# Two DFT steps along S, from 128x128 weights with masks to 32x32 tiles, in a forward and backward pass of a spectral mixer and a token MLP

## The chip, the cores and the metric

The kernel runs on one core of a Trainium2 chip (trn2), in one launch. The metric is the device time in microseconds (us), the median over several executions. TensorE is PE (its weight loads are listed as PEld), VectorE DVE, ScalarE ACT, GpSimd POOL, SyncE SP. SP issues nearly all DMAs.

## The reference

Inputs are bf16: `x` and `grad_out` of 2048 x 448 (S x D), the filter `w_r`, `w_i` of 2048 x 225, `w1` of 2048 x 1792, `w2` of 1792 x 2048, and the biases. With LN the layer norm over D:

```python
def _A_ref(x, w_r, w_i):                       # spectral filter
    X = jnp.fft.rfft2(x.astype(jnp.float32), axes=(-2, -1))
    X = X * (w_r + 1j * w_i)
    return jnp.fft.irfft2(X, s=(S, D), axes=(-2, -1)).astype(jnp.bfloat16)

def _B_ref(x, w1, b1, w2, b2):                 # MLP over the tokens
    h = LN(x)
    u = gelu(einsum("bsd,sf->bdf", h, w1) + b1)
    return (einsum("bdf,fs->bds", u, w2) + b2).transpose(0, 2, 1)

h  = x + _A_ref(LN(x), w_r, w_i)
h2 = h + _B_ref(LN(h), w1, b1, w2, b2)
# outputs: h2 and the gradients of x, w_r, w_i, w1, b1, w2, b2 for grad_out
```

## The kernel before

**Stages.** In the order of PE's work: (1) warm-up; (2) the forward DFT of LN(x) along D and the first step along S, a loop `for t in range(NT)` over 16 tiles with `row_a(t+1)` (4 matmuls of 128 columns) and `row_b(t-3)` (4 of 226); (3) `s2_stage`, the second step along S, the product with the filter and the first inverse step; (4) `inv_rows`, the rest of the inverse, and the layer norm of `h`; (5) the MLP forward and the gradients up to `dh` (the loop with `mm(pdh...)`), in which the first step of the backward DFT starts (`rows(t)`); (6) `s2_stage` again, for the gradient, with `bwd_mult`; (7) `inv_rows` again with `gx_consumer`, which makes the gradient of `x`; (8) what is left of the weight gradients.

**Fill.** Two long products have no place of their own: `dg_gen` (`w2` times `grad_out`, 224 matmuls of 448 columns) is fed into stages 2 and 3, and `gw_gen` (the gradients of `w1` and `w2`) into stages 5 to 8. Each is a Python generator; `fill(n)` emits its next n steps. A step of `dg_gen` is one matmul. Fourteen steps of `gw_gen` are twelve matmuls of 512 columns (in the last quarter of out_4, 256) and one group of four matmuls on 64 rows each (`parts`). What is left of `dg_gen` at the end of stage 3, and of `gw_gen` at the end of stage 7, is emitted there by `drain()`.

**Second step along S.** S = 16 x 128 frequencies lie in 16 groups of 128 rows. In each group the step is a 128x128 complex matrix which by the arrangement of the rows is nonzero only where a mask (`masks`, four comparisons per row) leaves it: the tables `Ut`, `Vt` are made as compact columns by ACT's Sin (`comp`), then spread over 128 columns by 16 multiplications with the mask columns (`gen_UV`). `UTt`, `VTt` are their permuted transposes, made on PE (`gen_inv_s`, 8 calls of four 128-column matmuls). In `s2_stage` a group takes three full matmuls forward and three back (`s2_inv`):

```python
mm(pv, lhsT=Vt[:, g, :], rhs=D2[:, g, :, :], start=True, stop=False)              # 452 columns
mm(pv[:, 0, :], lhsT=Ut[:, g, :], rhs=D2[:, g, 1, :], start=False, stop=False)    # 226
mm(pv[:, 1, :], lhsT=Un[g], rhs=D2[:, g, 0, :], start=False, stop=True)           # 226
evac(out=xs[c2][:, i, :, :], in_=pv, scale=scale)
```

The stage runs over pairs of groups `c2`. After each group comes `fill(n_fill)`: 3 in stage 3, 8 in stage 6. After each pair the filter product `w_mult` (4 DVE products) follows, in stage 6 also the filter's gradient (4 more). `D2` (the input of the stage) is written by 8 DMAs (L693), `D3` (its output) by one DMA per group (L756), each issued some PE time after the evacuation it stores (`defer`, `RESH_LAG`).

**Filter.** `w_load` (L583) reads `w_r`, `w_i` by eight DMAs in rows of up to 7200 bytes into `W_rows` (four in the loop of stage 2, four at the start of stage 3); `w_place` (32 copies) puts them in the order of the groups into `rG` during stage 3; a DMA stores them to DRAM (`w_d`, L963), and four DMAs (L1216) fetch them back into `rC` in stage 5. The gradient is stored from there by `w_io` (L572), eight DMAs.

**Who evacuates.** `evac` gives each PSUM tile to ACT or DVE by a planner's two loads (`Meter`, L62 to L81): each instruction adds its estimated cost, and neither load may fall behind the other by more than `Meter.slack` (2.0, in stage 6 4.0). PSUM has four buffers of the kind `ps_ff` (used by the DFTs) and four of `ps_mm` (used by the fill). PE, DVE, ACT and SP run in the order written down; POOL's order is the scheduler's.

Of the kernel before, what the change touches and what calls it, by code (L numbers as in the profile page):

```python
# [17 lines left out]
P = 128  # L18
# [104 lines left out]
def kernel(  # L123
# [98 lines left out]
    def v4(ap):  # L222
        return ap.rearrange("p (b c) -> p b c", b=4)
# [8 lines left out]
    r2 = region("r2", NG * 3 * KW)  # L232
# [3 lines left out]
    rX = region("rX", NG * 2 * KW)  # L236
    r452 = region("r452", 8 * 452)
# [4 lines left out]
    Ut = mem.tile([P, NG, P], BF16, name="Ut")  # L242
    Vt = mem.tile([P, NG, P], BF16, name="Vt")
    UTt = mem.tile([P, NG, P], BF16, name="UTt")
    VTt = mem.tile([P, NG, P], BF16, name="VTt")
# [3 lines left out]
    permI = mem.tile([P, P], BF16, name="permI")  # L249
# [35 lines left out]
    w_d = dram.tile([P, NG * 2 * KW], BF16, name="w_d")  # L285
# [70 lines left out]
    fr = ftmp(448, 64)  # L356
    gp_.iota(fr.rearrange("p (c q i g) -> p c q i g", c=2, q=2, i=4), pattern=[[1, 2], [8, 2], [16, 4], [2, 4]], base=0,
# [73 lines left out]
    def gen_R(ve, sc):  # L431
        t = ftmp(2688, P).bitcast(I32)
        tv = t.rearrange("p (c h x) -> p c h x", c=4, h=2)
        f2 = fr.rearrange("p (c x) -> p c x", c=4)
        for h in range(2):
            ve.tensor_scalar(out=tv[:, :, h, :], in0=f2, scalar1=pcol, scalar2=96.0 + 32.0 * h, op0=ALU.mult, op1=ALU.add)
        ve.tensor_scalar(out=tv[:, 0, 1, 0:1], in0=pcol, scalar1=64.0, scalar2=96.0, op0=ALU.mult, op1=ALU.add)
        ve.tensor_scalar(out=t, in0=t, scalar1=127, scalar2=None, op0=ALU.bitwise_and)
        sc.activation(out=Rm[:], in_=t, func=ACT.Sin, scale=s128, bias=half_r)


    def decode(eng):
        a4, fc, s_, c_, f_ = col(), col(), col(), col(), col()
        floor_div(eng, a4, pcolb, 32)
        gp_madd(s_, a4, -32.0, pcolb)
        floor_div(eng, fc, s_, 4)
        gp_madd(s_, fc, -4.0, s_)
        gp_madd(s_, s_, 4.0, a4)
        floor_div(eng, c_, fc, 4)
        gp_madd(f_, c_, -4.0, fc)  # L450
        return fc, s_, c_, f_

    def masks(eng, c_, f_):
        msk, mk, k0, k1 = col(4), col(), col(), col()
        for j in range(4):
            eng.tensor_scalar(out=msk[:, j:j + 1], in0=f_, scalar1=float(j), scalar2=None, op0=ALU.is_equal)
        eng.tensor_tensor(out=mk, in0=msk[:, 0:1], in1=c_, op=ALU.mult)
        eng.tensor_scalar(out=k1, in0=mk, scalar1=-1.0, scalar2=1.0, op0=ALU.mult, op1=ALU.add)
        eng.tensor_tensor(out=k0, in0=mk, in1=msk[:, 0:1], op=ALU.subtract)
        eng.tensor_scalar(out=k0, in0=k0, scalar1=1.0, scalar2=None, op0=ALU.add)  # L460
        return msk, mk, k0, k1

    comp_ring = ring(rO, 0, 2, 512)

    def gen_UV():
        _, s_, c_, f_ = rows = decode(gp_)
        nrow = col()
        gp_madd(nrow, rows[0], 16.0, s_)
        msk, mk, k0, k1 = masks(gp_, c_, f_)
        slf = col()  # L470
        gp_.tensor_tensor(out=slf, in0=s_, in1=f_, op=ALU.mult)
        gp_.tensor_scalar(out=slf, in0=slf, scalar1=16.0, scalar2=1536.0, op0=ALU.mult, op1=ALU.add)
        ou, ov0, ov1, pu, pv = col(), col(), col(), col(), col()
        gp_madd(ou, c_, 1536.0, slf)
        gp_madd(ov0, c_, -512.0, slf)
        gp_.tensor_scalar(out=ov0, in0=ov0, scalar1=512.0, scalar2=None, op0=ALU.add)
# [5 lines left out]
        ve.tensor_scalar(out=permI[:], in0=krow[:, 0:P], scalar1=nrow, scalar2=None, op0=ALU.is_equal)  # L482
        ve.scalar_tensor_tensor(out=base[:, 0, :, 1], in0=fix, scalar=mk, in1=base[:, 0, :, 1], op0=ALU.mult, op1=ALU.add)
        for dst, o0, o1, pt in ((Ut, ou, ou, pu), (Vt, ov0, ov1, pv)):
            t = ftmp(1024 if dst is Ut else 2048, 16, 16, 2).bitcast(I32)
            for k, o in ((0, o0), (1, o1)):
                ve.tensor_scalar(out=t[:, :, :, k], in0=base[:, :, :, k], scalar1=s_, scalar2=o,
                                 op0=ALU.mult, op1=ALU.add)
                yield
            ve.tensor_scalar(out=t[:, 0, :, 1], in0=base[:, 0, :, 1], scalar1=s_, scalar2=pt, op0=ALU.mult, op1=ALU.add)  # L490
# [3 lines left out]
            comp = comp_ring.next()  # L494
            sc.activation(out=comp, in_=t.rearrange("p g l c -> p (g l c)"), func=ACT.Sin, scale=s2048, bias=half_uv)
            yield True
            cv = comp.rearrange("p (g l c) -> p g l c", g=16, l=16)
            for c, k in ((1, k0), (0, k1)):
                ve.tensor_scalar(out=cv[:, 0, :, c], in0=cv[:, 0, :, c], scalar1=k, scalar2=None, op0=ALU.mult)
            yield  # L500
            d0 = dst[:, :, 0:64].rearrange("p g (l f) -> p g l f", f=4)
            d1 = dst[:, :, 64:112].rearrange("p g (l f) -> p g l f", f=3)
            for j in range(4):
                m = msk[:, j:j + 1]
                dj = d1[:, :, :, j - 1] if j else dst[:, :, 112:128]
                for o, c in ((d0[:, :, :, j], 0), (dj, 1)):
                    if load[1] + 0.24 < load[0] + 0.38:
                        ve.tensor_scalar(out=o, in0=cv[:, :, :, c], scalar1=m, scalar2=None, op0=ALU.mult)
                    else:
                        sc.activation(out=o, in_=cv[:, :, :, c], func=ACT.Copy, scale=m)  # L510
                    yield
# [7 lines left out]
    def gen_inv_s(h):  # L519
        src, dst = ((Ut, UTt), (Vt, VTt))[h // 4]  # L520
        g0 = 4 * (h % 4)
        pt = ps_ff()
        for i in range(4):
            mm(pt[:, i * P:(i + 1) * P], lhsT=src[:, g0 + i, :], rhs=permI[:], start=True, stop=True)
        evac(out=dst[:, g0:g0 + 4, :].rearrange("p g c -> p (g c)"), in_=pt[:])
# [34 lines left out]
    W_view_F = cut(rG, 0, NG, 2, KW)  # L560
    W_view_B = cut(rC, 0, NG, 2, KW)

    def w_io(Wv, dr, di, store):
        for c_, d in ((0, dr), (1, di)):
            for p0, p1, g0, g1, row, dims in ((0, 64, 0, 16, 0, [[16 * DF, 4], [1, 16 * DF]]),
                                              (64, 112, 0, 16, 112, [[-DF, 48], [1, DF]]),
                                              (112, 128, 1, 16, 127, [[-DF, 15], [1, DF]]),
                                              (112, 128, 0, 1, 64, [[1, DF]])):
                sb = Wv[p0:p1, g0:g1, c_, 0:DF]
                d_ap = bass.AP(d.tensor, d.offset + row * DF, [[P * DF, 16]] + dims)  # L570
                if store:
                    nc.sync.dma_start(out=d_ap, in_=sb)  # L572
                else:
                    nc.sync.dma_start(out=sb, in_=d_ap)
                yield

    W_rows = cut(rB, 0, 2, NG, DF)

    def w_load():
# [869 lines left out]
```

## Time and profile before

| | us |
|---|---|
| median of 3 runs | 356.51 |
| lowest, highest | 356.15, 356.75 |
| span of the profiled execution | 355.2 |
| PE busy in it | 340.1 (96%) |
| DVE busy | 253.9 (71%) |
| ACT busy | 214.9 (61%) |
| POOL busy | 69.7 (20%) |

For the profiled execution the page gives the span, from the first to the last instruction; its own time with what lies around the span is not listed apart. The three timed executions lie 1.0 to 1.6 us above it, the median 1.3 us, and that is taken as what lies around the span.

The page shows the busy time of each engine, then the span in 40 slices, then the chain of work that ended last, then the costliest groups of instructions. A matmul's own duration covers the way through the array, so matmuls overlap: what a matmul costs PE is the distance from its start to the next start, which the timeline gives. The granted clock is 1.00 in all stages.

### The profile page before, as it was taken

What the parts mean: (1) busy time and instruction counts of PE and PEld (TensorE: products, weight loads), DVE (VectorE), ACT (ScalarE), POOL (GpSimd) and SP (SyncE); (2) the same over time, 40 slices, a digit from 0 to 9 for tenths busy, and PEclk for the clock granted to TensorE, in tenths of its full rate; (3) what the DMA queues carried; (4) which work ended last, traced back from release to release, by engine and by line L of the source; (5) the groups of instructions that cost most, each with busy time, mean ns of one, the idle gap of its engine ahead of it and who ended that gap; (6) DMA issues with size and microseconds to landing.
All of it is one profiled execution on the core that took longest, in us unless ns stands there. A gap on an engine that the chain in (4) does not pass through costs nothing.

```text
span 355.2 us, 6479 instructions
## 1 busy us (share of the span) xinstructions
PE 340.1 (96%) x2147; PEld 184.2 (52%) x2147; DVE 253.9 (71%) x679; ACT 214.9 (61%) x458; POOL 69.7 (20%) x227
## 2 busy tenths in 40 slices
PE   7588999999999999999999999999999999999995
PEld 3355766555645555555555555544454544555642
DVE  8895638981884888776236988786595965499993
ACT  5469848964986545504322346666387766579872
POOL 6876000000220000001001111110000000067880
PEclk9999999999999999999999999999999999999999
DMA  8999979768999999997876999969966898799995
GB/s 196 284 190 244 212 186 184 139 170 279 285 288 352 297 350 230 246 235 213 209 171 149 184 219 190 206 158 304 295 177 193 231 233 248 230 198 284 209 303 221
DMA packets 147673, 81.64 MB, mean 230 GB/s; under 512 B 95480, under 2 KB 139768, under 8 KB 147384
## 3 DMA queue, kind: packets, MB, share of 16 engines
q1 hardware_dynamic: 147352, 80.83, 91.9%
q8 instruction: 17, 0.28, 0.3%
q10 hardware_dynamic: 288, 0.39, 0.3%
q14 instruction: 16, 0.13, 0.1%
HBM read 27.56 MB, written 23.89 MB: 145 GB/s over the span
## 4 chain that ended last, share of the span: by engine, by line
PE 82%; ACT 6%; POOL 5%; DVE 4%; issue 2%; DVEq 0%; ACTq 0%; POOLq 0%
PE ps_mm L218 68%; PE ps_ff L218 14%; ACT rO L82 2%; DVE r L82 1%; ACT rG L82 1%; ACT Ut L82 1%; DVE rA L82 1%; POOL cols L406 1%; POOL cols L407 0%; DVE rG L82 0%; ACT rX L82 0%; ACT rD L82 0%; ACT rAT L82 0%; ACT csI L82 0%; POOL nt_f L385 0%
## 5 line engine op out<-in xcount | busy, mean ns | idle before, releaser
L218 PEld LDWEIGHTS <-r 128*128 128x128 bf16 (+1 forms) x660 | 61.8, 104 | 50.0 <-issue 3.0
L218 PEld LDWEIGHTS <-rS 128*128 128x128 bf16 (+2 forms) x496 | 40.1, 97 | 37.8 <-issue 4.9
L218 PE MATMUL ps_mm<-rD,r 128*128 128x448 bf16 x224 | 44.5, 352 | 0.0
L82 ACT CAST rO<-ps_mm 128x512 bf16<-128x512 f32 (+1 forms) x66 | 35.2, 579 | 11.3 <-PE ps_mm L218 10.8
L218 PEld LDWEIGHTS <-rst 128*128 128x128 bf16 (+1 forms) x320 | 23.8, 97 | 29.0 <-issue 13.7
L218 PE MATMUL ps_mm<-rC,rE 128*128 128x448 bf16 x144 | 33.4, 352 | 3.2 <-DMA rC<-in_grad_out_dram 3.2
L218 PE MATMUL ps_mm<-r,rst 128*128 128x512 bf16 (+3 forms) x192 | 36.5, 353 | 0.0
L82 ACT CAST r<-ps_ff 128x452 bf16<-128x452 f32 x55 | 31.3, 577 | 7.3 <-PE ps_ff L218 6.2
L218 PE MATMUL ps_mm<-rB,r 128*128 128x448 bf16 x160 | 31.2, 352 | 0.1
L218 PE MATMUL ps_mm<-rG,rst 128*128 128x512 bf16 (+1 forms) x128 | 28.4, 380 | 0.0
L82 ACT ACTIVATE r<-ps_mm,rstd_h 128x448 bf16<-128x448 f32 x16 | 10.1, 634 | 26.8 <-PE ps_mm L218 26.8
L82 ACT ACTIVATE r<-rC 128x448 bf16<-128x448 bf16 x16 | 9.1, 570 | 26.7 <-DMA out_dram<-r 21.8
L82 DVE SCALAR_TENSOR_TENSOR r<-ps_mm,b2col,r 128x448 bf16<-128x448 f32 x16 | 10.9, 682 | 19.9 <-PE ps_mm L218 18.3
L82 ACT ACTIVATE rG<-rG 128x896 bf16<-128x896 bf16 x14 | 13.3, 950 | 14.9 <-DVE rG L82 14.7
L218 PE MATMUL ps_mm<-rE,rS 128*128 128x448 bf16 x112 | 21.5, 352 | 0.0
L218 PEld LDWEIGHTS <-rO 128*128 128x128 bf16 (+1 forms) x165 | 15.7, 98 | 10.9 <-ACT rO L82 0.2
L1179 POOL TENSOR_SCALAR lcol<-lcol 128x1 f32<-128x1 f32 x16 | 8.5, 532 | 64.7 <-ACT r L82 64.7
L82 ACT CAST rS<-ps_ff 128x512 bf16<-128x512 f32 x30 | 17.7, 592 | 4.3 <-PE ps_ff L218 4.3
L1370 POOL TENSOR_SCALAR lcol<-lcol 128x1 f32<-128x1 f32 x16 | 4.6, 287 | 76.5 <-ACT r L82 76.4
L218 PEld LDWEIGHTS <-rE 128*128 128x128 bf16 x148 | 14.0, 98 | 10.6 <-issue 3.7
L218 PE MATMUL ps_ff<-csI,rAT 113*128 113x224 bf16 (+1 forms) x108 | 19.0, 297 | 0.4 <-ACT rAT L82 0.2
L82 ACT CAST rG<-ps_mm 128x512 bf16<-128x512 f32 (+1 forms) x28 | 14.4, 550 | 8.1 <-PE ps_mm L218 8.0
(196 smaller groups left out, 667.0 us busy)
## 6 DMA issues: line engine op xcount, KB each, us to landing
out_dram<-rO SPq DMA_DIRECT2D x34, 256.0 KB
r<-in_B_w_dram SPq DMA_DIRECT2D x5, 1024.0 KB
r<-r SPq DMA_DIRECT2D x16, 226.0 KB
r<-r SPq DMA_DIRECT2D x32, 113.0 KB
rS<-in_B_w_dram SPq DMA_DIRECT2D x4, 896.0 KB
out_dram<-rG SPq DMA_DIRECT2D x10, 256.0 KB
rO<-in_B_w_dram SPq DMA_DIRECT2D x2, 1024.0 KB
w_d<-rG SPq DMA_DIRECT2D x1, 1808.0 KB
```

The source lines that it names most:

```text
L82: fn(**kw)
L218: nc.tensor.matmul(out, lhsT=lhsT, rhs=rhs, start=start, stop=stop)
L406: gp_.tensor_scalar(out=gtmp, in0=in0, scalar1=scalar, scalar2=None, op0=ALU.mult)
L1179: gp_.tensor_scalar(out=m1, in0=ms, scalar1=-1.0 / D, scalar2=None, op0=ALU.mult)
L1370: gp_.tensor_scalar(out=m1, in0=ms, scalar1=-2.0 / D, scalar2=None, op0=ALU.mult)
```

## The change

The rows are arranged in such a way that the second step's matrix is block diagonal in blocks of 32 within each group. The tables are 32 columns wide and need no masks (`masks` and its 16 multiplications are gone; the angles get two more DVE operations, `bi`). `s2_stage` takes the groups in four sets of four. For each of the three tables a set issues 16 matmuls with 32x32 weights, one for each block row r and each group a; group a's block r lands in rows r + a (modulo 4), so that the 16 use all 16 places of the array. Forward, `fill(n1)`, back for the set before, product, `fill(n2)` follow for each set. The filter is loaded in place into a tile of its own, `rW`, by `w_io` (18 DMAs with rows of 450 bytes, all in the loop of stage 2) and stays there, so that `w_place`, `w_d` and the four loads are gone; its gradient is stored by the same 18 patterns. `gen_inv_s` is 4 calls of 32 small matmuls. The fill is dealt out anew. The diff, cut to its core:

```diff
+    def small(out, lhsT, rhs, start, stop):
+        nc.tensor.matmul(out, lhsT=lhsT, rhs=rhs, start=start, stop=stop)
+        clock[0] += int(np.prod(rhs.shape[1:])) / 38400.0
+    def blk(i):
+        return slice(32 * i, 32 * i + 32)
+    def set_groups(s):
+        return [8 * (s // 2) + s % 2 + 2 * a for a in range(4)]
...
+    Ut, Vt, Un, UTn = (mem.tile([P, NG, 32], BF16, name=n) for n in ("Ut", "Vt", "Un", "UTn"))
+    UVT = mem.tile([P, 2, NG, 32], BF16, name="UVT")
...
     def gen_UV():
...
+        ve.tensor_scalar(out=bi, in0=base, scalar1=i16, scalar2=None, op0=ALU.add)
+        ve.tensor_scalar(out=bi, in0=bi, scalar1=2047 - 64, scalar2=None, op0=ALU.bitwise_and)
+        yield
...
-            for j in range(4):
-                m = msk[:, j:j + 1]
-                dj = d1[:, :, :, j - 1] if j else dst[:, :, 112:128]
-                for o, c in ((d0[:, :, :, j], 0), (dj, 1)):
-                    if load[1] + 0.24 < load[0] + 0.38:
-                        ve.tensor_scalar(out=o, in0=cv[:, :, :, c], scalar1=m, scalar2=None, op0=ALU.mult)
-                    else:
-                        sc.activation(out=o, in_=cv[:, :, :, c], func=ACT.Copy, scale=m)
-                    yield
...
-        for i in range(4):
-            mm(pt[:, i * P:(i + 1) * P], lhsT=src[:, g0 + i, :], rhs=permI[:], start=True, stop=True)
+        for w, src in enumerate((Ut, Vt)):
+            for x in range(4):
+                o = 32 * (4 * w + x)
+                for r in range(4):
+                    small(pt[blk(r + a & 3), o:o + 32], lhsT=src[blk(r), 8 * (x // 2) + 2 * a + x % 2, :], rhs=permI[blk(r), :],
+                          start=True, stop=True)
...
+    def w_io(dr, di, store):
         for c_, d in ((0, dr), (1, di)):
+            for i in range(4):
+                for p0, g0, g1, row, dims in ((0, 0, 16, 16 * i, [[DF, 16], [1, DF]]),
+                                              (16, 0 if i else 1, 16, 128 - 16 * i - (not i), [[-DF, 16 if i else 15], [1, DF]]),
+                                              (16, 0, 1, 64, [[1, DF]])):
+                    if i and row == 64 and g1 == 1:
+                        continue
+                    p0 += 32 * i
+                    sb = W[p0:p0 + 16, g0:g1, c_, 0:DF]
+                    d_ap = bass.AP(d.tensor, d.offset + row * DF, [[P * DF, 16]] + dims)
+                    nc.sync.dma_start(out=d_ap if store else sb, in_=sb if store else d_ap)
                     yield
...
+    def s2_stage(get_x, on_mult, n1, n2, gap, after=None, scale=None):
         flush()
+        def four(tables, s, turn, rhs):
+            gs = set_groups(s)
+            ps = [ps_ff()[:, 0:452].rearrange("p (c k) -> p c k", c=2) for _ in gs]
+            for t, c, start, stop in ((tables[0], None, True, False), (tables[1], 0, False, False), (tables[2], 1, False, True)):
+                for a, g in enumerate(gs):
+                    for r in range(4):
+                        x, o = rhs(a, g, r), ps[a][blk(r + turn * a & 3)]
+                        small(o if c is None else o[:, c, :], lhsT=t[blk(r), g, :], rhs=x if c is None else x[:, 1 - c, :],
+                              start=start, stop=stop)
+            run_due()
+            return ps
+        y = None
+        for s in range(5):
+            if s < 4:
+                x = get_x(s)
+                for a, pv in enumerate(four((Vt, Ut, Un), s, 1, lambda a, g, r: D2[blk(r), g])):
+                    evac(out=x[:, a], in_=pv, scale=scale)
+            fill(n1)
+            if s:
+                for g, pv in zip(set_groups(s - 1), four((VTt, UTt, UTn), s - 1, -1, lambda a, g, r: y[blk(r), a])):
+                    ab = r452_ring.next()
+                    evac(out=ab, in_=pv)
+                    defer(RESH_LAG, lambda g=g, ab=ab: nc.sync.dma_start(out=D3[rowbase(g):rowbase(g) + 29:4, :, :, :], in_=ab), ab)
+            if s < 4:
+                y = Y_ring.next()
+                for j in range(2):
+                    on_mult(s, j, x[:, 2 * j:2 * j + 2], y[:, 2 * j:2 * j + 2])
+            if after is not None and s in after:
+                after[s]()
+            fill(n2)
         fill(gap)
...
-    FILL_A = (4, 4, 4, 3, 3, 4, 4, 4, 4, 4, 4, 3, 3, 3, 3, 3)
-    FILL_B = (0, 0, 0, 3, 3, 3, 3, 3, 3, 3, 3, 3, 3, 3, 3, 3)
+    W_AT = {4: 1, 5: 1, 6: 1, 7: 1, 8: 2, 9: 2, 10: 2, 11: 2, 12: 2, 13: 2, 14: 2}
+    FILL_A = (4, 4, 4, 3, 3, 3, 3, 3, 3, 3, 3, 3, 3, 3, 3, 3)
+    FILL_B = (0, 0, 0, 2, 2, 2, 2, 2, 2, 2, 2, 2, 2, 2, 2, 2)
...
-    wp = w_place()
-    fill(14)
+    gen_inv_d(0)
+    fill(6)
+    gen_inv_d(1)
...
-    s2_stage(fwd_x, fwd_mult, ML_F, 3, 24, True)
+    s2_stage(lambda s: set_of(Xs, s), fwd_mult, 10, 14, 0)
+    sc.activation(out=warm, in_=eps_h, func=ACT.Sqrt)
+    fill(24)
     drain()
-    nc.sync.dma_start(out=w_d[:], in_=rG[:, 0:NG * 2 * KW])
...
-    s2_stage(bwd_x, bwd_mult, 0, N_FILL_B[3], N_FILL_B[4], False, {5: lambda: load_du(0), 9: lambda: load_du(1), 13: lambda: load_du(2)}, 2.0 * INV_SD)
+    s2_stage(lambda s: X_ring.next(), bwd_mult, 14, 22, N_FILL_B[4], {1: lambda: load_du(0), 3: lambda: (load_du(1), load_du(2))},
+             2.0 * INV_SD)
...
-    GW_AT = (1, 3, 5, 6, 7, 9, 11, 12)
+    GW_AT = tuple(range(1, 13)) + tuple(range(6, 12))
```

In the changed program the planner deals the evacuations of stage 6 as follows: in DVE's queue, between the products of one set and those of the next, stand one or two evacuations of the set's forward step, two of the fill, and one or two of the back step of the set before; before the first set's products stand three forward ones and two of the fill. In stage 3 two of the four back evacuations of each set stand on DVE between the products of two sets; the forward ones are on ACT but for two of the first set.

## The prediction

> **What bounds the kernel now.** I read, in this order: the page's shares, the slices, the chain, then PE's timeline at the step that changes, and the queues around it.
>
> ```profile
> PE 340.1 (96%) x2147; PEld 184.2 (52%) x2147; DVE 253.9 (71%) x679; ACT 214.9 (61%) x458; POOL 69.7 (20%) x227
> PE   7588999999999999999999999999999999999995
> PE 82%; ACT 6%; POOL 5%; DVE 4%; issue 2%; DVEq 0%; ACTq 0%; POOLq 0%
> ```
>
> PE is busy 96% of the span, its slices are full from the fifth on, and 82% of the chain is PE. So what is taken from PE's own time shortens the run, unless a queue that PE's time used to cover comes out. PE's timeline shows one group of the second step, then the fill:
>
> ```profile
> 49.74 0.35 PE L218 MATMUL ps_ff<-r,Vt 128*128 128x452 bf16 x1
> 49.93 0.26 PE L218 MATMUL ps_ff<-r,Ut 128*128 128x226 bf16 x1
> 50.02 0.26 PE L218 MATMUL ps_ff<-r,r 128*128 128x226 bf16 x1
> 50.12 0.35 PE L218 MATMUL ps_mm<-rC,rE 128*128 128x448 bf16 x1
> ```
>
> From start to start a group takes 50.12 - 49.74 = 0.38 us. Two stages of 16 groups, forward and back, are 64 of these: 24.4 us, or 12.2 per stage. Sixteen sets take their place, one for every four groups.
>
> **What a set costs.** Nothing before runs on 32x32 weights. The nearest rows are the matmuls on 64 rows, PE's timeline again:
>
> ```profile
> 289.07 0.26 PE L218 MATMUL ps_ff<-rS,r 128*128 128x226 bf16 x1
> 289.26 0.61 PE L218 MATMUL ps_mm<-rG,rS 64*128 64x512 bf16 x4
> ```
>
> In single rows the first two of the four start 3 ns apart, so two halves of the array, different rows of it, do work side by side. The change of shape costs: 0.19 us from 289.07 to 289.26 where 226 columns need 0.096, so 0.095 more, and as much on the way out: 0.19 in all. If sixteen places work as two do, each table streams its columns once for four groups, and a set lasts as one group did: 0.38 + 0.19 = 0.57. If the 96 instructions (48 weight loads, 48 matmuls) take 3 ns each and none of it hides, 0.86. No row shows two matmuls on the same rows of the array but other columns; if these go one after the other, four turns make 4 x 0.38 + 0.19 = 1.71. If nothing runs side by side, the nearest rows are the 128-column pairs of load and matmul, 0.056 apart: 48 x 0.056 + 0.19 = 2.9. I take 0.75, between the first two, since the 64-row rows are the nearest in kind. Four groups cost 1.52 before; with the stalls that I find below, the change gains nothing from a set of about 1.3 on.
>
> The weight loads' rows bear on the third bound: the four loads of that group of four began with the first matmul and were done in 0.11 us, while the first two still streamed on the rows that the last two were to use.
>
> ```profile
> 289.26 0.11 PEld L218 LDWEIGHTS <-rS 64*128 64x128 bf16 x4 [0.19 <-issue]
> ```
>
> The Trainium skill ("TensorE: Matmul & The Clock Gate", section "The mechanism") says against the change that a weight load overlaps running matmuls only where the rows of the array differ (its background buffer aside), by which, as an estimate, a set would be 1.71 and the whole some 361; the loads above did overlap on the same rows. The same page's table of measured packings has sixteen 32x32 places at 10.6 times one, as if nothing of the kind bound. Its section "Wait — 56ns, not 53.3ns?" says that starts are never closer than about 25 ns, an estimated 48 x 25 ns + 0.19 = 1.39 a set and 358 in all; the 3 ns above contradict that for different rows, and no row here decides for sixteen places.
>
> **A. Up to the last `row_b` (PE at 46.30 before).** 19 steps of `dg_gen` leave the loop: 19 x 0.189 = 3.6 us earlier, though not saved, as they return in stage 3. The mask multiplications go. ACT's and PE's timelines:
>
> ```profile
> 27.04 1.93 ACT L82 ACTIVATE Ut<-rO,cols 128x256 bf16<-128x256 bf16 x3
> ```
>
> ```profile
> 29.45 0.56 PE L218 MATMUL ps_ff<-csF,rS 112*128 112x226 bf16 x4 [1.48 <-ACT rS L82]
> ```
>
> PE stood from 27.6 to 29.45 for an evacuation that ACT did after three of them, 1.65 us more than the matmul before needed: gone. The two `bi` operations of 512 elements (some 0.4 each) on DVE stand ahead of a tile's copy at 19 to 21 us, when PE already waits: +0.8. `gen_inv_s` moves within the loop: half of its 32 matmuls of 128 columns were there (16 x 0.056 = -0.9), and its 4 calls of 32 small ones of 32 columns cost 0.19 for the mode and 32 x 2 x 3 ns = 0.38 at most in all: 0.35, so +1.4. PE's last `row_b` ends at 46.30 - 3.6 - 1.65 + 0.8 - 0.9 + 1.4 = 42.4.
>
> **B. SP, the wait that appears.** SP's timeline before:
>
> ```profile
> 29.62 2.03 SPq L297 DMA_TRANSPOSE rE<-in_B_w_dram  x1
> 35.53 1.32 SPq L583 DMA_DIRECT2D rB<-in_A_w_r_dram  x2
> 40.31 7.32 SPq L693 DMA_DIRECT2D r<-r  x4
> ```
>
> SP issues in order, a load in 0.5 to 0.66 us, a store of `D2` (L693) in 0.57, a transpose in 2.0 to 2.5, and at 28.8 us it is some 6 us behind its due times; before, it caught up at 40 and waited for PE, which the long 7.32 shows. Now 18 loads of the filter instead of 4 stand in this queue among the stores. From 28.8: 18 x 0.5 + 8 x 0.57 + 2 x 2.2 = 18 us, so the last store goes out at 46.5 and lands some 1.7 later. Stage 3's first set waits for it: it starts at about 48.3, against 49.74, though PE was done at 42.4; of the 5.9 in between `fill(6)` and `gen_inv_d` cover some 2, PE idles 4. Behind this wait stands all of PE's queue. Free of it the stage starts at about 44.5; three us more of it if 450-byte packets hold the queue (the page already has 95480 of 147673 packets under 512 B, with the DMA engines 92% busy). The skill ("DMA: Bandwidth & Descriptors", its specifications) puts line rate from 512 bytes on; no row here shows a load of 450 apart.
>
> **C. Stage 3.** PE saves 32 x 0.38 - 8 x 0.75 = 6.2, and takes the 19 fill steps and 8 that stood just ahead of it. The stalls of 0.94, 0.43 and some 0.6 before, behind `w_place` copies on ACT and DVE, are gone (-1.9). But products now come in lumps: on DVE one set's four products of two pairs take 2 x 1.95 = 3.9 us, then the back step (0.85) must run and two evacuations of 0.62 follow: 6.0 a set, against PE's 2 x 0.75 + 24 x 0.189 = 6.04. Level: no stall to count, none to spare. The 16 `gen_inv_s` matmuls just ahead (-0.9) go as well. From 48.3, eight steps of 0.75 and the 141 fill steps left (26.6) come to 80.9; with 0.6 for the last lump of DVE 81.5, against 86.1: **-4.6**. With SP in time, from 44.5, it would be -8.4, of which I count -7, since DVE's level cycle would then show; with SP three us later it is -1.6.
>
> **D. Stage 6.** The same 6.2 from PE. Here a set has eight products, DVE's timeline:
>
> ```profile
> 275.98 1.16 DVE L82 TENSOR_TENSOR rS<-rS,rC 128x904 bf16<-128x904 bf16 x2
> 277.18 0.70 DVE L82 TENSOR_TENSOR rS<-rS 128x452 bf16<-128x452 bf16 x2
> 277.91 1.17 DVE L82 TENSOR_TENSOR rS<-rS,rX 128x904 bf16<-128x904 bf16 x2
> 279.12 0.70 DVE L82 TENSOR_TENSOR rC<-rS 128x452 bf16<-128x452 bf16 x2
> ```
>
> One pair of groups is 3.93 from the first row to the last one's end, a set 7.85. In DVE's queue four to six evacuations of 0.62 to 0.69 stand between two sets' products, 2.6 to 3.9: a cycle of up to 11.75, against PE's 36 steps of 0.23 (14 steps of `gw_gen` are 3.22) + 1.5 = 9.8. PE waits where a fill's or a back step's evacuation stands behind products: by hand 0.2 in the second set, 1.4 and 1.3 in the third and fourth, +2.9 (none if ACT, 0.80 of whose time here is busy, takes them in time; 5 if each cycle is lost in full). **-6.2 + 2.9 = -3.3**.
>
> **E. The rest.** The 1.8 MB store `w_d` and its loads go; `h`'s own queue gains a little, -0.3. Eight stores of the filter's gradient become 18, in stage 7, on SP, with the stores of the inverse:
>
> ```profile
> L572 SPq DMA_DIRECT2D out_dram<-rC x8: 422/627/1414, 309.9 to 339.7; - x8
> ```
>
> Ten more at 0.63 are 6 us of a queue with waits in it; PE's end hangs on other things, so 0 to +2: +0.5. Negatives of 32-column tables are small. In sum -4.6 - 3.3 - 0.3 + 0.5 = -7.7: span 355.2 - 7.7 = 347.5, and 1.3 around it (the profiled execution stands as the median does): **349 us**.
>
> **The rivals.**
> First, all sixteen places dense and SP in time: C gives -7, D -4.7 with half of its stalls: 356.5 - 7 - 4.7 - 0.3 + 0.5 = 345, and 343 with sets of 0.57. For it: the 3 ns rows and a queue that before caught up by 40. Against it: the sum of issues in B.
> Second, the stalls are larger: SP three us later (C -1.6) and D with stalls of 5 (-1.2): 356.5 - 1.6 - 1.2 - 0.3 + 0.5 = 354. For it: DVE's cycle above PE's, and the packets.
> Third, the other side, and the change not doing what it says: places on the same rows of the array don't run side by side. A set of 1.71 instead of 0.75 adds 16 x 0.96 = 15.4; as PE is then slower than DVE, the stalls of C and D go (-0.6 - 2.9): 349 + 15.4 - 3.5 = 361; with a set of 1.6, 359. With nothing side by side, 2.9 a set, it is some 380. It decides from a set of 1.3 us. For it: 96 instructions for each twelve matmuls, and no row with two places on the same rows. Against it: the 3 ns, and the loads that overlapped.
>
> **How the numbers follow.** Forecast 349: 0.44. Dense, 345: 0.21. More stalls, 354: 0.18. Places in turn, 361: 0.17. The range reaches from 343 to 360, which leaves out the larger part of the last case, 0.13, and 0.05 below the first's low end. A measurement here tells 0.2%, 0.7 us, from no change. Of the case of more stalls 0.04 falls within that and 0.02 above it, of the last case 0.01 within it. Faster: 0.44 + 0.21 + 0.18 - 0.06 = 0.77; the same: 0.04 + 0.01 = 0.05; slower: 0.17 - 0.01 + 0.02 = 0.18.
>
> **What would show it.** A set from its first to its first other start: 0.6 to 0.9 on PE, starts a few ns apart. The first set near 48, PE idle before it, released by a DMA into `D2`, with SP's queue full to then. No mask work at 27 us. In stage 6 PE's idle time with DVE's evacuations as its releaser, some 3 us. Wrong: sets over 1.3; a stage 3 that starts before 45 or after 50; the end set by SP's stores.

## The result and the profile after

The changed kernel took 371.11 us (median of 4, 366.88 to 373.44) against 356.63 before, a ratio of 1.037 with an interval of 1.031 to 1.043: 14.5 us slower, where 349 was forecast and 343 to 360 given. The profiled execution is the longest of the four, 373.44 with a span of 371.3; it counts as slow, being over 1.5% above the fastest, and without it, as in the ratio, the median is 370.15, 13.5 us above before. What lies around the span is 2.1 us, 0.8 more than before.

The page's shares, PE's slices and granted clock, and the chain, after:

```profile
PE 334.9 (90%) x2819; PEld 174.3 (47%) x2819; DVE 256.6 (69%) x677; ACT 192.3 (52%) x421; POOL 68.3 (18%) x220
PE   8669731999799999999999999999999989899993
PEclk9999955899989999999999999999999999999998
PE 62%; DVE 13%; DMA 11%; issue 4%; POOL 4%; ACT 2%; SPq 2%; DVEq 0%; ACTq 0%; POOLq 0%
```

PE has a hole in the sixth and seventh slice (3, 1), its clock falls to half there, and DMA, not on the chain at all before, holds 11% of it. PE's timeline in the hole, and one set of the second step later in the stage:

```profile
42.15 1.74 PE L218 MATMUL ps_ff<-csF,rS 112*128 112x226 bf16 x16
...
43.91 0.35 PE L218 MATMUL ps_mm<-rC,rE 128*128 128x448 bf16 x1
49.41 0.58 PE L545 MATMUL ps_ff<-ident,csF 128*113 128x128 bf16 x4 [5.14 <-ACT r L82]
49.78 2.44 PE L218 MATMUL ps_mm<-rC,rE 128*128 128x448 bf16 x6
52.02 0.63 PE L545 MATMUL ps_ff<-ident,csF 128*113 128x128 bf16 x4
63.52 0.82 PE L223 MATMUL ps_ff<-r,Vt 32*32 32x452 bf16 x16 [10.87 <-DMA r<-r]
...
70.79 0.41 PE L223 MATMUL ps_ff<-r,Vt 32*32 32x452 bf16 x16
70.99 0.30 PE L223 MATMUL ps_ff<-r,Ut 32*32 32x226 bf16 x16
71.17 0.39 PE L223 MATMUL ps_ff<-r,Un 32*32 32x226 bf16 x16
71.50 0.74 PE L218 MATMUL ps_mm<-rC,rE 128*128 128x448 bf16 x3
```

A set takes 71.50 - 70.79 = 0.71 us. But the first one waits for a DMA into `D2` until 63.52, and from 44.1 to then PE does only some 3 us of work. Cut at the starts of the matmuls that open each part, in us, the forecast from the steps of the prediction:

| part | before | forecast | after |
|---|---|---|---|
| up to the first set of stage 3 | 49.74 | 48.3 | 63.52 |
| stage 3, to the first `RTm` matmul | 36.37 | 33.2 | 36.56 |
| stage 4 and the MLP, to `rows` | 112.63 | 112.3 | 114.15 |
| `rows` to stage 6 | 52.08 | 52.1 | 52.17 |
| stage 6, to the next `RTm` | 54.02 | 50.7 | 55.59 |
| stage 7, to its last `RTm` | 31.82 | 31.8 | 31.84 |
| from there to PE's last matmul | 14.65 | | 10.87 |
| from there to the end of the span | 3.89 | | 6.64 |

The differences add up to the 16.1 us between the spans: 13.8, 0.2, 1.5, 0.1, 1.6, 0, -3.8 and 2.7. In two other runs with the same front the first set starts at 60.9 and 62.3, so 11.1 and 12.6 later than before instead of 13.8.

The 13.8 are in SP's timeline, in the chain (start, length) and in ACT's timeline, after:

```profile
46.77 3.23 SPq L571 DMA_DIRECT2D rW<-in_A_w_i_dram  x4
50.63 0.54 SPq L669 DMA_DIRECT2D r<-r  x1
51.52 4.22 SPq L571 DMA_DIRECT2D rW<-in_A_w_i_dram  x4
55.84 1.83 SPq L669 DMA_DIRECT2D r<-r  x3
```

```profile
46.19 7.74 DMA r<-r
54.02 0.06 ACT r L82
56.48 6.95 DMA r<-r
```

```profile
48.82 0.54 ACT L82 CAST r<-ps_ff 128x452 bf16<-128x452 f32 x1 [7.74 <-DMA r<-r]
```

The last store of `D2` is issued at 57.1, some 11 us later than forecast, and the last three land 7 us after their issue instead of 1.7. In the kernel before, the eight stores landed 2.2 to 7.2 us after their issue, the last one 2.7. A landing also frees one of the four buffers of `cs_ring`, for which the evacuation of a later row waits: the store issued at 42.44 lands at 48.72 and lets ACT's evacuation start at 48.82, which is PE's wait for ACT at 49.41; the store issued at 46.19 lands at 53.92 and lets the last row's evacuations start at 54.02, ahead of the last stores.

The clock's row in the windows after (span of the window, its length, busy us of PE, PEld, DVE, ACT, POOL, clock, DMA share, GB/s):

```profile
47.00:49.00 2.00, 0.00 (x0) 0.00 (x0) 0.19 (x1) 0.18 (x1) 0.00 (x0) 0.55 1.29 83
65.00:67.00 2.00, 2.00 (x7) 0.85 (x6) 1.97 (x5) 0.64 (x2) 0.00 (x0) 0.50 0.98 221
67.00:69.00 2.00, 2.00 (x11) 0.91 (x10) 1.86 (x5) 0.53 (x1) 0.00 (x0) 0.83 0.35 76
```

The clock is down some 3 us after PE's last matmul and back 4 us after work starts again. The first set takes 64.67 - 63.52 = 1.15 us instead of 0.71 and the 24 fill steps behind it 6.12 instead of 4.54: 2.0 us. A second dip from 102 to 105 us, behind a wait of 2.0 us for the last `D3` store, fits the 1.5 of stage 4: from the end of stage 3 to stage 6 the runs without a dip there take 164.7 to 165.4 us, this one 166.3. The Trainium skill ("TensorE: Matmul & The Clock Gate", Part 1) has the clock at half after about 3.4 us without work and back after as much of it; the rows of the first dip agree within a microsecond. The second dip came though PE had worked 1.5 of the 3.4 us before it, which that rule by itself does not give.

### The profile page after: what moved, and what is told of

It reads as the page before. It is cut to its first block, busy times and chain, and to the rows that moved or that the text cites. A ratio compares the mean times of both kernels' runs of the same rounds, so it can differ in the third digit from the quotient of the medians.

```text
span 371.3 us, 7810 instructions
## 1 busy us (share of the span) xinstructions
PE 334.9 (90%) x2819; PEld 174.3 (47%) x2819; DVE 256.6 (69%) x677; ACT 192.3 (52%) x421; POOL 68.3 (18%) x220
## 4 chain that ended last, share of the span: by engine, by line
PE 62%; DVE 13%; DMA 11%; issue 4%; POOL 4%; ACT 2%; SPq 2%; DVEq 0%; ACTq 0%; POOLq 0%
PE ps_mm L218 51%; PE ps_ff L218 8%; DVE r L82 8%; DMA r<-r 6%; PE ps_ff L223 3%; DVE rS L82 2%; DMA r<-rD 2%; DMA out_dram<-r 1%; DMA rS<-rB 1%; SPq L571 1%; ACT r L82 1%; ACT rO L82 1%; DMA out_dram<-rO 1%; SPq L1169 1%; POOL cols L415 0%
## 5 line engine op out<-in xcount | busy, mean ns | idle before, releaser
L218 PEld LDWEIGHTS <-r 128*128 128x128 bf16 (+2 forms) x600 | 56.3, 106 | 48.7 <-issue 6.6
L82 ACT CAST rO<-ps_mm 128x512 bf16<-128x512 f32 (+1 forms) x61 | 33.0, 578 | 16.7 <-PE ps_mm L218 14.1
L82 ACT CAST r<-ps_ff 128x452 bf16<-128x452 f32 x42 | 23.4, 586 | 21.0 <-DMA r<-r 12.4
L82 DVE CAST r<-ps_ff 128x452 bf16<-128x452 f32 x22 | 13.4, 630 | 21.9 <-DMA r<-r 13.8
L82 ACT CAST rAT<-ps_ff 113x512 bf16<-113x512 f32 x24 | 14.0, 590 | 12.4 <-PE ps_ff L218 12.4
L1137 POOL TENSOR_SCALAR lcol<-lcol 128x1 f32<-128x1 f32 x16 | 8.5, 529 | 64.7 <-ACT r L82 64.7
L82 ACT CAST rG<-ps_mm 128x512 bf16<-128x512 f32 (+1 forms) x33 | 16.3, 536 | 7.4 <-PE ps_mm L218 7.3
```

Source lines behind the costliest of these rows:

```text
L82: fn(**kw)
L218: nc.tensor.matmul(out, lhsT=lhsT, rhs=rhs, start=start, stop=stop)
L1137: gp_.tensor_scalar(out=m1, in0=ms, scalar1=-1.0 / D, scalar2=None, op0=ALU.mult)
```

## Experiments: what holds stage 3 back

**No loads.** Edit: `w_loads = iter(())`, `W` filled by a POOL memset.

> The changed kernel without the 18 loads of the filter (the filter is filled with zeros on chip, so the products and the gradients that depend on it are left without it); all else as changed. Theory P (packets): the 4096 packets of 450 bytes keep the 16 DMA engines, so the stores of D2 land 7 us after their issue instead of 1.7. Theory Q (issues): the 18 issues in SP's order keep D2 back. Both expect stage 3 to start at 45 to 47 us instead of 63.5, its first fill steps at the full clock, and 349 to 352 us in all against 371. If the start stays above 55, neither holds, and D2's stores or the row evacuations are late for a reason of their own.

Measured: 357.46 us, stage 3 from 50.66. The start is 13 us earlier, but neither the 45 to 47 nor the 349 to 352 us that both theories expected. The memset took 6.1 us of POOL at 2.3 and put the first rows off (PE waited 5.5 us before 14.98, and the last `row_b` group starts 4.5 us later than in the changed kernel), so that the 13 us gained hold 4 to 5 lost in front. The loads are the cause; how much of it is packets was left to the next.

**Long rows, the same 18 issues.** Edit: destination `rW[p0:p0 + 16, ...]` contiguous over 16 rows, source `[[P * DF, 16], [1, 16 * DF]]`.

> The changed kernel with the same 18 loads, at the same places in SP's order, onto the same partitions and with the same bytes, but in rows of 7200 bytes instead of 450 (the filter then lies in another order in its tile, so that the product takes wrong values). Theory P (packets): the D2 stores land in some 2 us, stage 3 starts at 47 to 51, 351 to 356 us. Theory Q (issues): 18 issues are 18 issues; the start stays at 58 to 63 and the time at 366 to 371.

**Two issues.** Edit: `dma_start(out=rW[:, 3616 * c_:...], in_=d.rearrange("(p t) f -> p (t f)", t=16))`, twice.

> The changed kernel with two loads of the filter onto all 128 partitions in rows of 7200 bytes instead of 18 (the same bytes; the filter lies in another order, so that the product takes wrong values). The run with 18 long rows had stage 3 start at 54.0; what two issues instead of 18 take from that is the issues' share. If the issues hold SP for their 0.5 us each (16 x 0.5 = 8), the start is 46 to 48 and the time 351 to 354 us. If the bytes themselves in busy DMA engines make the rest, the start stays at 51 to 54 and the time at 357 to 361.

Measured: start 54.03 and 360.73 us with 18 loads of long rows, between the two theories, and 48.39 and 355.18 with two loads. So of some 15 us, 9.5 come with the packets (63.5 to 54.0; 7 to 8 by the two other runs with the same front, at 60.9 and 62.3) and 5.6 with the 16 issues more. These 5.6 are not the issues' time alone: the two loads also write 128 partitions each instead of 16 and are done by 36.8 us instead of 52.1. Both theories hold a part, packets the larger. The windows of the two runs, first the changed kernel, then the one with two loads:

```profile
45.00:50.00 5.00, 0.59 (x5) 0.53 (x5) 0.63 (x1) 0.54 (x1) 0.10 (x1) 0.72 1.03 96
```

```profile
30.00:35.00 5.00, 5.00 (x72) 3.48 (x71) 2.90 (x12) 4.04 (x10) 3.71 (x17) 1.00 1.03 319
```

At the same share of the DMA engines, full, the first moves 96 GB/s and the second 319; in the first a quarter of the engines' time goes to stores of `D2`. By packet, the 4096 of 450 bytes took 62 ns each on average, which is 15.9 us of all 16 engines, and with two loads the 256 of 7200 bytes took 347 ns, 5.6 us. The difference, some 10 us, is near what comes out. A packet's time also holds what it waits for others, so this is an account and no proof.

How full engines hold SP back shows in SP's waits after (us in total, times, longest):

```profile
SPq L571 <- DMA r<-r: 2.2, 2, 1.4
SPq L571 <- DMA rW<-in_A_w_i_dram: 1.5, 2, 1.2
```

The program's DMAs, SP's and ACT's alike, take eight completion semaphores in turn. From 48.7 to 55.4 us each of SP's issues starts within 0.1 us of the landing of the transfer that had its semaphore before: 48.74 after 48.72, 53.94 after 53.92, 55.43 after 55.41. With eight under way SP goes at the pace of the landings, so that packets and issues are not two separate prices.

**Another queue.** Edit: the loads by `nc.scalar.dma_start`.

> The changed kernel with the 18 loads of 450-byte rows issued from ACT's queue instead of SP's, at the same places in the program. Theory Q (issues): SP is free for D2, the start of stage 3 is 46 to 49, 351 to 355 us, less what ACT loses by 18 issues. Theory P (packets): the same packets lie in the same 16 engines, D2's stores still land 4 us or more after their issue; start 55 to 62, 362 to 371 us.

Measured: 368.6, start 61.97. SP was free of the loads, the DMA engines were not: as theory P says. SP was not wholly free, though: some of its last stores still waited for a semaphore that a load of ACT's had (53.72 after 53.65).

**Fewer, larger loads, put in order by masks.** Edit: 12 loads to a staging tile, six of them (three of the four blocks, real and imaginary part) of the form `[[(113 - 32 * i) * DF, 2], [P * DF, 16], [1, 16 * DF]]`, then `T * m + reversed(T) * (1 - m)`; the second with 12 + 20 fill steps in stage 6.

> The changed kernel with the filter loaded by 12 DMAs in rows of 7200 bytes onto 16 or 32 partitions of a staging tile and put in its order on chip: by a mask for the rows that run forward and one for those that run backward (ACT and DVE for the first two sets before stage 3, ACT and POOL for the others in it). By packets and issues as the runs so far have them, stage 3 starts at 48 to 51, between two and 18 long-row loads; 355 to 358 us. If the masks' work on ACT and DVE (some 1.7 us a set and engine) comes out in stage 3, 358 to 361.

> The kernel with the staged filter and with 12 + 20 fill steps per set in stage 6 instead of 14 + 22. Theory T (tail): 3 to 4 us less than the staged one alone, 351 to 355 us. If PE's sum sets the end: the same as that.

Measured: 389.92 and 390.19, the start at 74.8 and 73.5. Neither expectation came near; the window of the first shows why:

```profile
35.00:40.00 5.00, 3.40 (x89) 2.31 (x87) 2.03 (x6) 2.08 (x5) 0.24 (x2) 1.00 0.12 52
```

With 2 as the slowest dimension the loads run on about two of the 16 engines (0.12), at 52 GB/s, and everything behind them waits. The skill ("DMA: Bandwidth & Descriptors", "Why a DMA increments its semaphore by 16 and not by 1") says that the number of engines is the largest up to 16 that divides the slowest dimension of both sides; this agrees.

**Loads moved behind `D2`.** Edit: loads by halves of the groups, 11 of 34 in the loop, the rest behind `flush()`, eight fill steps ahead of `gen_inv_d`, slack 6 in stage 3, and the two edits of stage 6 below.

> The changed kernel with the loads of 450-byte rows split by halves of the groups (34 of half the size); 11 of them stand in the loop, the others behind the last store of D2, so that the stores of D2 have fewer packets before them and the first two sets need only the first half; slack 6 in stage 3, and the two edits of stage 6. If packets ahead of D2 are what made stage 3 late, it starts at 48 to 52 with the clock at 1.00. If the bound is the DMA engines' time as such (18 times 1.4 us for the filter), the wait comes out behind the first products instead, and stage 3 ends at 88 to 92 instead of 100; 355 to 359 us. If it is not, 351 to 354.

Measured: 363.87, above both expectations; start 49.50 with the clock at 1.00, but stage 3 took 45.5 us and ended at 95. PE's timeline (the wait in brackets) and SP's:

```profile
75.00 0.36 PE L218 MATMUL ps_mm<-rC,rE 128*128 128x448 bf16 x1 [3.65 <-DMA rE<-in_B_w_dram]
...
95.03 0.76 PE L218 MATMUL ps_ff<-RTm,r 128*113 128x128 bf16 x5 [7.68 <-DMA r<-r]
```

```profile
62.86 5.43 SPq L584 DMA_DIRECT2D rW<-in_A_w_i_dram  x8
68.39 6.08 SPq L306 DMA_TRANSPOSE rE<-in_B_w_dram  x2
74.57 2.89 SPq L712 DMA_DIRECT2D r<-r  x4
```

The front is repaired, the bill comes later: the first set's `D3` stores stand behind loads and transposes. Two runs asked whether that is SP's order.

> The kernel with the loads split by halves, and in stage 3 the stores of D3 are issued by ACT instead of SP, and the two transposes of the biases go behind the stage. In the run before, the first set's D3 stores stood 14 us behind loads and transposes in SP's queue, and the last landed at 94.7, 8 us after PE had run out of fill. Theory S (SP's order): with a queue of their own stage 3 ends at 86 to 88 instead of 95, with the clock at 1.00, and the time is 353 to 356 us. Theory M (the DMA engines' time): the stores wait in the engines as they did in SP's queue; the end stays at 92 or later, 360 to 364 us.

> The same with the 18 loads of the changed kernel instead of 34 of half the size: 8 in the loop, 10 behind the last store of D2. The first product then needs the whole filter. By the DMA engines' time (10 loads at 1.4 us and two transposes from 48 on) it starts at 64 to 67 instead of 54, four cycles of 4.5 to 6 us follow, and stage 3 ends at 88 to 92; 355 to 360 us. If 16 issues less on SP weigh more than that, it is not later than the one with halves.

Edits: `D3` stores by `nc.scalar`, `turn_biases()` behind the stage; in the second 18 loads, 8 of them in the loop. Measured: 369.99 and 370.9, stage 3 52.5 and 54.4 us long. ACT's timeline in the first, and its chain:

```profile
87.44 7.39 ACTq L712 DMA_DIRECT2D r<-r  x2
```

```profile
79.92 14.21 DMA r<-in_B_w_dram
```

Theory S falls; theory M has the direction, not the size (stage 3 ends at 99.7 and 104.7). The second of these two issues of `D3` starts at 94.21, with the landing, at 94.14, of a `w1` load of 1 MB that SP had issued at 79.92 on the same semaphore, and ACT's evacuations stood behind it. What it would be with semaphores that ACT does not share with SP was not tried.

## Experiments: stage 6 and the end

**No gradient stores.** Edit: `g_out = iter(())`.

> The changed kernel without the 18 stores of the filter's gradient (those two outputs are left out). The first part is as changed. If these stores are what holds the stores of x's gradient near the end (5.45 us from issue to landing, DVE waiting for their buffer), the 6.6 us from the last matmul's start to the end of the span fall to about 4 and the time to 367 to 369. If the end hangs on DVE's own work on the last tiles, it stays at 370 to 372.

Measured: 367.78, as the first theory has it, but not for its reason: the stretch behind PE's last matmul only fell from 6.64 to 5.94, while the start of stage 3 (60.9) and a wait for `D3` behind stage 6 came out better, both ahead of the place of these stores. So the first theory has the time by luck, and ten more stores are worth 0.7 us at most.

**Fewer fill steps in stage 6**, against the kernel with two loads. Edit: `s2_stage(..., bwd_mult, 12, 20, ...)`.

> As the kernel with two loads, and in stage 6 each set is followed by 12 + 20 fill steps instead of 14 + 22, so that 20 steps (4.3 us) move from there to behind stage 7. Theory T (tail): the end follows stage 7 by what DVE and the stores still have to do for x's gradient, 16.8 to 18 us in all runs, with PE done 6 us before the end; then stage 6 is 3 to 4 us shorter and so is the whole. If PE's sum of work sets the end, the time stays; if DVE's cycle sets stage 6, that stays at 53.7 to 55 us, and the time with it.

Measured: 355.39 against 355.18. Stage 6 fell from 55.3 to 53.5 though PE had some 4 us less to do in it, and behind stage 7 PE's longer rest (14.65 + 3.9 us instead of 10.87 + 6.2) took back 1.5 of the 1.8. Theory T falls; that DVE sets stage 6 fits, and the next run tests it.

**The planner's slack.** Edit on top: `Meter.slack = 12.0` in stage 6 instead of 4.0.

> As the kernel with two loads and 12 + 20 fill steps (355.4), and the planner's slack in stage 6 is 12 instead of 4. With 4 the planner forgets what of a set's 7.85 us of products goes beyond 4 us of ACT's lead and deals evacuations to DVE, which was 94% busy there with 35 us for three and a half sets. With 12 three of them are left on DVE between the products. Theory D (DVE's cycle sets stage 6): 7.85 + 0.6 a set instead of 11 leaves PE's 8.9, stage 6 falls from 53.5 to 49 or 50, the whole to 351 or 352. Rival: ACT, which takes what DVE loses (8 us a set), becomes as late as DVE was; stage 6 stays above 52 and the time at 354 to 356.

Measured: 351.33 (ratio 0.986, 0.982 to 0.991), stage 6 50.46. Stage 6 as a whole in the windows of the kernel before, the changed one, the one with fewer fill steps and the one with slack 12 as well (DVE is the third busy time, ACT the fourth):

```profile
250.81:304.83 54.02, 54.02 (x307) 25.23 (x306) 37.55 (x76) 37.02 (x73) 0.00 (x0) 1.00 0.82 230
```

```profile
266.40:321.99 55.59, 52.68 (x618) 21.20 (x617) 45.96 (x92) 31.88 (x62) 0.00 (x0) 1.00 0.81 224
```

```profile
250.30:303.76 53.46, 48.11 (x588) 19.37 (x595) 45.08 (x90) 31.10 (x60) 0.00 (x0) 1.00 0.79 215
```

```profile
248.39:298.85 50.46, 48.95 (x596) 19.37 (x595) 36.56 (x75) 37.53 (x75) 0.00 (x0) 1.00 0.88 238
```

The change gave DVE 8.4 us more work and ACT 5.1 less: DVE has 28 evacuations where it had 12, ACT 61 where it had 73. DVE is busy for 46.0 of 55.6 us over the stage, and in its middle (275.4 to 311.0) for 34.1 of 35.6. A set's products are a lump of 7.85 us on DVE; the planner forgets a lead of over 4 us, so ACT counts as caught up long before it is, and evacuations go to DVE and stand behind the products. With slack 12 DVE is back at 36.6 with 11 evacuations, and PE's gaps come to 1.5 us.

> The changed kernel with these two edits in stage 6 alone (slack 12, 12 + 20 fill steps); its outputs are the reference's. By theory D 4 us less than the changed kernel, 365 to 368; if ACT is as late, 369 to 372. The first 100 us are as in the changed kernel.

> The kernel before with the planner's slack 12 in stage 6 instead of 4 and nothing else. Theory D says that the slack matters only where the products come in lumps of 7.85 us; here they come in lumps of 3.9 us with 74% of DVE busy and PE without a gap, so the time stays within 0.5 us of 356.5. If the slack by itself were the gain, stage 6 (54.0) would fall here too, by 2 us or more.

The two edits in the changed kernel: 367.27, stage 6 49.99 instead of 55.59, as theory D says. The slack alone in the kernel before: 356.86 against 356.36, stage 6 54.02 as ever. So the slack is no gain by itself, and the loss comes with the sets; that it is the size of their lumps fits both runs, but no run made the lumps smaller. The whole gained 3 to 4 us, less than the stage, since behind stage 7 it took 18.56 instead of 17.51.

## Experiments: the true filter in long rows

**Order made on PE.** Edit: two loads as above into `rB`, then for each group two matmuls by 0/1 matrices and one evacuation, `mm(o, lhsT=pm[:, 0], rhs=N[:, :, g])`, `mm(o, lhsT=pm[:, 1], rhs=N[:, :, NG - g])`, and both edits of stage 6.

> A whole kernel again, with the reference's outputs: the filter comes by two loads of 7200-byte rows on all 128 partitions, as in the run with two loads, and PE puts it in its order, with two matmuls by a permutation matrix and one evacuation for each group (32 matmuls of 450 columns, 32 x 0.19 = 6.1 us), three sets of it ahead of stage 3, where PE waits some 3.5 us for D2, the last inside; slack 12 and 12 + 20 fill steps in stage 6. The run with two loads and these edits took 351.3 us. If PE's wait covers what stands in it: 6.1 - 3.5 = 2.6 more, 353 to 355 us, under the 356.4 of before. If the evacuations (12 of 0.55 to 0.63) hold up the last rows' evacuations: 356 to 358.

> The same with two sets placed ahead of stage 3 and two inside, and the planner's slack 6 instead of 2 in stage 3, where a set's lump of products is 3.9 us. If DVE's evacuations behind the products cost something in stage 3 as they did in stage 6, it is 1 to 2 us less than the one before, 352 to 354; if stage 3 is set by PE and the landing of D3, the same as the one before.

Measured: 360.41 and 358.68, above all that was expected. The 6.1 us were hidden in part only: stage 3 began at 52.1 and 51.1, and PE stood still for evacuations ahead of it. In the second stage 3 took 39.1 us instead of 37.8; 1.5 of it are the set more that is placed inside, so that slack 6 shows no gain, and its own part was not measured apart.

**Order of the work, then buffers.** Edits: `place(0); gen_inv_d(0); place(1); gen_inv_d(1); place(2)`; then `cs_ring` with eight buffers in the forward pass.

> The kernel that orders the filter on PE, slack 6 in stage 3, with the tables of the inverse (csI) made between the placed sets instead of behind them, three sets placed ahead of stage 3 and no fill there. In the run with two sets ahead, PE waited 1.5 us for the last rows' evacuations and 1.8 us for csI's. If the order hides csI's evacuations, stage 3 starts at 51 to 52 with the placing of one set left, and takes 36 to 37 us instead of 39.1; 355.5 to 357 us, level with 356.5. If the rows' evacuations hold all of it, 358 to 360.

> The kernel before it in this row (filter ordered on PE, csI between the sets, 356.9), with eight buffers instead of four for the rows' evacuations on their way to D2 (cs_ring, in the forward pass). There PE stood still from 45.4 to 47.6 for an evacuation on ACT, behind one that waited for the landing of an earlier D2 store, since its buffer held that store's data. Without that wait stage 3 starts at 51 to 52 instead of 54.1, the rest as it was: 353 to 355 us, under the 356.5 of before. If the landing of D2 itself is what PE waits for, 356 to 357.

Measured: 356.85, level with 356.49 before, though not as expected: stage 3 starts at 54.1 instead of 51 to 52 and is shorter for it (35.5 us). Then 354.31 (ratio 0.995, 0.993 to 0.997), the only kernel with the filter in its right order that beats both, by half a per cent. PE's timeline of the one with four buffers and of that with eight:

```profile
47.55 0.98 PE L218 MATMUL ps_mm<-rB,rG 128*128 128x450 bf16 x4 [2.15 <-ACT rD L82]
```

```profile
44.05 1.71 PE L218 MATMUL ps_mm<-rB,rG 128*128 128x450 bf16 x8
45.59 0.39 PE L545 MATMUL ps_ff<-ident,csF 128*113 128x128 bf16 x4
...
50.54 0.41 PE L223 MATMUL ps_ff<-r,Vt 32*32 32x452 bf16 x16
```

The wait of 2.15 us for ACT is gone and stage 3 starts at 50.54 instead of 54.10. This execution, though, is the longest of its twelve (357.78): 1.6 us of the start are lost again in stage 3 (37.0) and 1.5 in stage 4, where the clock is at half for 3.4 us from 89.3. So the gain of 2.5 us in the median is measured, but no trace shows where it stays.

## Why the prediction was wrong

- **The set was right.** 0.75 us was taken, 0.71 measured, so the rival on the other side, by places that take turns (1.71), falls, though its sign came true. The sixteen matmuls of the first table start 3.3 ns apart, and so do the second's. The floor of 25 ns in the Trainium skill ("TensorE: Matmul & The Clock Gate", "Wait — 56ns, not 53.3ns?") does not hold across places, the 4 ns per tile of its Part 3 does for these two tables; the third's start 8.3 ns apart.
- **A was about right.** PE's last `row_b` group starts at 42.15 and is through its starts at 43.7; 42.4 was forecast, so it is 1.3 us late. The stall behind ACT's mask multiplications at 27.6 is gone: the longest wait of PE from 24 to 44 us is 0.3.
- **B is the step that failed**, with -1.4 forecast and +13.8 measured (11.1 and 12.6 in two other runs with this front). The mechanism, `D2` behind the loads in SP's queue, was named, and a start after 50 stood there as a sign of being wrong; its price was not seen. The sum gave SP 18 us to the last store: the loads 9, two transposes 4.4, the stores 4.6. SP took 28.2, from 29.5 to 57.7: the loads 15.0, the transposes 6.6, the stores 4.7 and 1.9 between them. The landing was put at 1.7 and took 7.0; 1.7 was below each of the eight landings of before (2.2 to 7.2). The 4096 short packets were weighed against 95480 that the page had under 512 bytes, as if those left room for them, with engines 92% busy. The runs put in its place 7 to 9.5 us that come with the packets and 5.6 with the issues. The case of more stalls, with three us for it, had the direction and a fifth of the size. What was not thought of: the eight semaphores, by which a late landing holds SP; `cs_ring`'s four buffers, which pass a late `D2` store on to the rows; and the clock, which charged 2.0 us in stage 3 and 1.5 in stage 4.
- **C, 33.2 forecast and 36.56 measured.** Half clock 2.0, the wait for the last `D3` store 2.0. With two loads it was 34.9, 0.9 of it such a wait.
- **D, -3.3 forecast and +1.6 measured**, is the second step that failed. DVE's cycle of 11.75 us was seen, but its stall was sized by hand at 2.9 with 5 as the worst. And the 22 fill matmuls more in this stage (232 against 210, some 3.9 us) were left out: the sum took PE's saving as if the steps stayed, and gained nothing in their new place. Slack 12 with 20 steps fewer, which leaves the 210 fill matmuls of before, gives the 50.5 of the forecast's 50.7.
- **E, +0.5 forecast.** Behind stage 7 it is 17.51 us against 18.54. The fill that went to stage 6 shortened PE's rest by 3.8, and DVE's work on `x`'s gradient, once for 5.45 us behind a store, took 2.7 of it back.

With the filter in two long-row loads (in a wrong order) and stage 6 dealt anew, most of the forecast gain comes out: 351.33 where 349 was forecast. With the filter in its right order 354.31 is the best that was measured.

## What to carry to other kernels

Price a load by its packets at a time when the engines are full, not only by its bytes and its issue: 450-byte rows cost nearly three times what 7200-byte ones did here (15.9 us of the 16 engines against 5.6), and the price fell on whatever was queued behind. When work is made coarser, look at what deals out the work around it: a planner whose slack of 4 us did for lumps of 3.9 us gave DVE 22% more to do with lumps of 7.85. Time taken from PE is worth what the next resource leaves: follow each saving to the stage's own limit before adding it up.

## What the runs showed of the hardware that was not expected

- With the eight semaphores of this program an issue stands still until the transfer that last had its semaphore has landed, on ACT's queue as on SP's: 7.39 us for two issues on ACT, with that engine's evacuations behind them, the second at 94.21 after a landing at 94.14.
- A landing is the last of sixteen completions, and one can be late by itself: of the `D2` store issued at 42.44, fifteen had come by 45.33 and the last came at 48.72.
- Between the first and the last microseconds of a run the half clock lasts a multiple of 3.4 us in all traces here: 3.4, 6.8, 10.2, 13.7 or 20.5.
- A POOL addition of 900 elements (1.93 us) held DVE's products up: 3.56 us for two of 452 elements that take 0.70 alone, in the run with masks. At the other place where POOL added, at 94.35, it was 3.55. The first:

```profile
82.67 3.83 POOL L599 TENSOR_TENSOR rW<-rG 128x900 bf16<-128x900 bf16 x2 [26.00 <-ACT rG L82]
```

```profile
83.19 3.56 DVE L82 TENSOR_TENSOR rS<-rS 128x452 bf16<-128x452 bf16 x2
```

- The third table's matmuls of a set start 8.3 ns apart, the first two tables' 3.3. The weight loads show a difference: in the set at 70.79 the second table's sixteen loads are issued by 70.89, 0.1 us ahead of its matmuls, while fifteen of the third's sixteen go out between its matmuls, 8.3 ns apart too. Why they don't run ahead was not tried.
